# An attention and channel-mixing kernel on Trainium2: every weight chunk's first shift stays in SBUF, under a new written order

## The chip, the cores and the metric

The kernel runs on one core of a Trainium2 chip. The metric is the device time of one execution in microseconds; lower is better. The profile is one execution taken by the hardware profiler. Engines are named as it names them: PE (matrix products), PEld (its weight loads), DVE (VectorE), ACT (ScalarE), POOL (GpSimd) and SP (SyncE, which here only issues transfers).

## What is computed

The reference is windowed attention (8 batches, 8 heads, 576 positions, head size 64, each position sees itself and 63 before it), whose output feeds a mixing layer with two hidden products:

```python
scores = np.where(mask, scale * q @ k.T, -1e9)
x = softmax(scores) @ v                      # 8 x 576 x 512 after joining the heads
x_prev = x shifted by one position
xk = mu_k * x + (1 - mu_k) * x_prev
xr = mu_r * x + (1 - mu_r) * x_prev
v = np.maximum(xk @ w_k, 0) ** 2 @ w_v       # 512 -> 1024 -> 512
out = sigmoid(xr @ w_r) * v
```

The three weight matrices reach the chip as 64-bit floating-point numbers, looked at as two 32-bit words each. The kernel makes 32-bit floats of them with integer operations.

## The kernel before

Positions are cut into nine units of 512 (`u` 0 to 8, eight attention blocks of 64 positions each). A unit has four groups, one for each pair of heads (`g` is 4u plus the pair). A group runs scores on PE (`run_s`), row minima on DVE (`least`), exponentials on ACT (`exp`), reciprocals of the row sums on DVE (`shares`), the multiplication by them on DVE or POOL (`scale`), a transposition (`turn` on DVE, or a flip on PE for the first four groups), and products with the values on PE (`values`, `whole_values`). Two groups from the second unit on share one pass of `values` on PE, called a values pass below; it has 80 products. The results are copied to tile `xT`. Then `mix` blends each position with the one before (`diff`, `blend`, `seam`), and PE runs the r, k and v products of the unit.

Products with 512 columns come in two kinds. The first unit's r and k products use the decoded weight as it is (`whole`, with `xm`): one product each, which the trace shows as two MATMUL records. All others use weights and data that are each split into a rounded high part and a rest (`ws` with `xs` or `ks`): three products for each. The split is `first_part` (a cast) and `second_part` (a subtraction) for weights, `high` and `low` for data.

The weights come in 20 chunks of 128 x 512 (tile `raw`): 0 to 3 are w_r, 4 to 11 w_k, 12 to 19 w_v. `decode` handles one chunk: `sign` on ACT (absolute value of the upper words), `clamp` on DVE or POOL, then on DVE `shift` (upper word left by three bits, masked), `top` (sign and top exponent bit put back) and `low` (three bits of the lower word put in). A table `FAST` says chunk by chunk where the shift writes:

```python
def shift(e):
    words[n, 0] = words[n].bitcast(U32) if FAST[n] else bank(WC).bitcast(U32)
...
def top(e):
    shifted = words[n, 0]
    if FAST[n]:
        words[n, 0] = bank(WC).bitcast(U32)
```

With 0 the shift reads SBUF (tile `wt`) and writes a PSUM bank, and `top` works in that bank. With 1 the shift stays in `wt` in SBUF, and `top` reads `raw` and `wt`, both in SBUF, and writes the bank.

What stands where on each engine is decided while the program is built. Each step is a numbered piece; the table `ORDER` gives for each engine the numbers of the first pieces in the order in which they are to stand, for the first unit and the beginning of the second. A planner (`play`) sets the rest by keys. A piece that may run on more than one engine runs on the one in whose list it stands. So `ORDER` also moves work between engines, and it orders the transfers on SP. `PLACES` names five values passes (numbered by pair of groups, 2 to 17) ahead of which PE's instruction stream is aligned to 256 with an offset of 7, if at most `SKIP` (12) empty instructions do it.

Of the kernel before, what the change touches and what calls it, by code (L numbers as in the profile page):

```python
# [70 lines left out]
MIX = ((-90, -68, -101, -111), (-40, -47, -16, -60))  # L71
LOADS = ("q0", "w", "q1", "v0", "w", "q2", "v1", "w", "v3", "m", "q3", "v2", "w", "w", "w", "w", "w")

FAST = (0, 0, 0, 0, 0, 0, 1, 0, 0, 1, 0, 0, 0, 1, 0, 0, 0, 1, 0, 0)
MIX1 = ((-24, -66, -65, -47), (16, 60, 62, 49))

SELF = {"DVE": 125, "ACT": 140, "POOL": 100, "PE": 0, "SP": 0}
LINK = {"DVE": 125, "ACT": 135, "POOL": 90, "PE": 205, "SP": 80}
FAR_LINK = 45

PLACES, SKIP = {3: 7, 4: 7, 8: 7, 12: 7, 16: 7}, 12

RING = 8
FIRST = 730
# [4 lines left out]

ORDER = {  # L90
# [9 lines left out]
    ),  # L100
    "DVE": (
# [11 lines left out]
    ),  # L113
    "ACT": (
# [10 lines left out]
    ),  # L125
    "POOL": (
# [4 lines left out]
    ),  # L131
# [7 lines left out]
    ),  # L139
}  # L140

# [6 lines left out]
def attn_rwkv_kernel(ctx, tc, qT, kT, v2, mu_k, mu_r, w_k, w_v, w_r, out):  # L148
# [189 lines left out]
    def bank(*shape):  # L338
        return psum.tile([P, *shape], F32, name="bank")
# [81 lines left out]
    def decode(n, loaded):  # L421
# [11 lines left out]
        def shift(e):  # L433
            words[n, 0] = words[n].bitcast(U32) if FAST[n] else bank(WC).bitcast(U32)
            dve.tensor_scalar(words[n, 0], words[n].bitcast(U32), 3, 0x3FFFFFF8,
                              op0=ALU.logical_shift_left, op1=ALU.bitwise_and)
# [27 lines left out]
        p = Piece({"DVE": 335, "POOL": 605}, key, 0, clamp, [p], port=True)  # L464
        if FAST[n]:
            p = Piece("DVE", key, 335, shift, [p], port=True)
# [743 lines left out]
```

## Time and profile before

| What | us |
|---|---|
| median of three runs | 607.07 |
| lowest and highest run | 606.57, 607.09 |
| the profiled execution, its own time | 607.59 |
| its span, first to last instruction | 605.8 |
| PE busy in the span | 593.6 |
| DVE busy | 391.1 |
| ACT busy | 371.3 |
| POOL busy | 133.9 |

The span is 1.27 us less than the median of the runs and 1.8 us less than the profiled execution's own time; what lies around it is start and end of the execution. PE's records overlap their neighbours, so its busy time contains short waits within a run of products; where a products run matters, it is read from the start of one record group to the start of the next.

### The profile page before, as it was taken

The numbers are of one execution on the slowest core, as the hardware profiler recorded it, in microseconds if no ns is written. First come the engines' busy times: TensorE is split into PE (matmuls) and PEld (weight loads), VectorE is DVE, ScalarE is ACT, GpSimd is POOL, SyncE is SP. The second block draws the span as 40 slices with busy tenths as digits, with TensorE's granted clock in tenths as the row PEclk, the third lists the DMA queues.
The fourth block names the chain that finished last, engine by engine and source line by source line (L and its number), as shares of the span: only waits on it lengthen the run. The fifth ranks groups of instructions, "written<-read, shape, count | busy, mean of one in ns | idle before, by whom it ended". The sixth has DMA issues, their size and how long they took to land.

```text
span 605.8 us, 17561 instructions
## 1 busy us (share of the span) xinstructions
PE 593.6 (98%) x7008; PEld 464.7 (77%) x7008; DVE 391.1 (65%) x1210; ACT 371.3 (61%) x1057; POOL 133.9 (22%) x205
## 2 busy tenths in 40 slices
PE   5999999999999999999999999999999999999997
PEld 4644577888888888888888888887888888888885
DVE  5999999737782768366754677277828683665211
ACT  6898967475576646673577358645865476743620
POOL 6665546202300330022101130023002300201000
PEclk9999999999999999999999999999999999999999
DMA  8988133213221323122312222132212220010001
GB/s 276 320 287 282 47 88 105 80 45 107 83 77 46 93 75 97 40 82 63 110 40 57 88 83 66 41 110 81 75 46 93 92 81 24 3 53 18 0 18 52
DMA packets 56913, 53.32 MB, mean 88 GB/s; under 512 B 10496, under 2 KB 50432, under 8 KB 56832
## 3 DMA queue, kind: packets, MB, share of 16 engines
q1 hardware_dynamic: 56832, 52.20, 28.2%
q8 instruction: 56, 0.92, 0.6%
q14 instruction: 25, 0.20, 0.1%
HBM read 42.73 MB, written 9.44 MB: 86 GB/s over the span
## 4 chain that ended last, share of the span: by engine, by line
PE 84%; DVE 6%; ACT 4%; DMA 3%; SPq 1%; issue 1%; POOL 1%; ACTq 0%
PE bank L168 84%; DVE bank L168 1%; DMA raw<-w_k 1%; ACT pr L168 1%; SPq L168 1%; DMA v<-v 1%; DMA raw<-w_r 1%; DVE xm L168 1%; ACT ws L168 1%; DVE wt L168 1%; ACT kf L168 1%; DVE d L168 1%; DVE r L168 0%; DVE whole L168 0%; DVE pt L168 0%
## 5 line engine op out<-in xcount | busy, mean ns | idle before, releaser
L168 PE MATMUL bank<-xs,ws 128*128 128x512 f32 x1152 | 272.7, 396 | 0.0
L168 PEld LDWEIGHTS bank<-xs,ws 128*128 128x128 f32 x1152 | 215.8, 188 | 51.0
L168 PE MATMUL bank<-ks,ws 128*128 128x512 f32 x864 | 206.8, 398 | 0.1
L168 PEld LDWEIGHTS bank<-ks,ws 128*128 128x128 f32 x864 | 161.3, 188 | 39.5 <-issue 1.0
L168 DVE TENSOR_TENSOR ks<-kf,ks 128x512 fp32r<-128x512 f32 x70 | 51.3, 734 | 93.7 <-ACT ks L168 93.5
L168 ACT ACTIVATE pr<-pr,nmax 128x96 f32<-128x96 f32 (+1 forms) x288 | 105.2, 368 | 8.8 <-DVE nmax L168 8.3
L168 ACT ACTIVATE kf<-bank 128x512 f32<-128x512 f32 x72 | 43.0, 598 | 61.1 <-PE bank L168 60.7
L168 DVE CUSTOM_DVE_ANT_0 pr<-bank,bands 128x96 f32<-128x96 f32 x256 | 49.5, 250 | 14.3 <-PE bank L168 14.3
L168 POOL CAST ks<-kf 128x512 fp32r<-128x512 f32 x7 | 4.3, 612 | 244.9 <-ACT kf L168 206.0
L168 ACT COPY xT<-bank 128x256 f32<-128x256 f32 (+1 forms) x43 | 14.5, 392 | 67.0 <-PE bank L168 67.0
L168 ACT ACTIVATION_READ_ACCUMULATOR pr<-pr,nmax 128x1 f32 x288 | 54.5, 189 | 0.0
L168 ACT ACTIVATE kf<-kf 128x512 f32<-128x512 f32 x71 | 44.8, 633 | 2.0
L168 ACT ACTIVATE th<-bank 128x512 f32<-128x512 f32 x36 | 21.3, 591 | 38.5 <-PE bank L168 27.2
L168 DVE SCALAR_TENSOR_TENSOR r<-bank,r 128x512 f32<-128x512 f32 x36 | 24.4, 680 | 31.4 <-PE bank L168 31.3
L168 PE MATMUL bank<-xm,whole 128*128 128x512 f32 x96 | 43.1, 599 | 0.0
L168 ACT CAST ks<-kf 128x512 fp32r<-128x512 f32 x65 | 40.3, 620 | 2.1 <-POOL kf L168 0.3
L168 PE MATMUL bank<-qk 64*32 64x96 f32 (+1 forms) x2112 | 33.4, 254 | 7.8 <-DMA qk<-kT 5.2
L168 PEld LDWEIGHTS bank<-qk 64*32 64x32 f32 (+1 forms) x2112 | 28.2, 108 | 15.9 <-DMA qk<-qT 5.2
L168 PEld LDWEIGHTS bank<-pt,v 32*64 32x64 f32 (+1 forms) x2656 | 34.3, 130 | 7.0 <-issue 5.0
L168 ACT CAST xs<-d 128x512 fp32r<-128x512 f32 x49 | 28.8, 618 | 15.3 <-POOL d L168 13.7
L168 DVE TENSOR_TENSOR xs<-d,xs 128x512 fp32r<-128x512 f32 x57 | 37.3, 698 | 0.4 <-ACT xs L168 0.4
L168 DVE COPY xT<-bank 128x256 f32<-128x256 f32 x26 | 10.3, 421 | 42.2 <-PE bank L168 42.2
(79 smaller groups left out, 562.0 us busy)
## 6 DMA issues: line engine op xcount, KB each, us to landing
v<-v SPq DMA_DIRECT2D x68, 64.0 KB, 2.0
raw<-w_k SPq DMA_DIRECT2D x8, 512.0 KB, 8.4
raw<-w_v SPq DMA_DIRECT2D x8, 512.0 KB, 6.0
v<-v SPq DMA_DIRECT2D x60, 48.0 KB, 2.0
raw<-w_r SPq DMA_DIRECT2D x4, 512.0 KB, 4.8
outT<-r SPq DMA_DIRECT2D x8, 256.0 KB, 2.0
v<-v SPq DMA_DIRECT2D x60, 32.0 KB, 1.9
qk<-kT SPq DMA_DIRECT2D x8, 224.0 KB, 3.7
```

Of the source, the lines that this page charges most:

```text
L168: self.last = tc.keep_in_program_order(op(*args, **kw))
```

## The change

`FAST` is 1 for all 20 chunks instead of four of them (6, 9, 13 and 17). `ORDER` is another table for all five engines; its written part is a little longer on PE. `PLACES` names passes 3, 4, 7, 11 and 15 instead of 3, 4, 8, 12 and 16. The r and k products of the first unit keep their undivided weights (`DIRECT = "rk"` stands in both). No operation is added or taken away.

```diff
-FAST = (0, 0, 0, 0, 0, 0, 1, 0, 0, 1, 0, 0, 0, 1, 0, 0, 0, 1, 0, 0)
+FAST = (1, 1, 1, 1, 1, 1, 1, 1, 1, 1, 1, 1, 1, 1, 1, 1, 1, 1, 1, 1)
...
-PLACES, SKIP = {3: 7, 4: 7, 8: 7, 12: 7, 16: 7}, 12
+PLACES, SKIP = {3: 7, 4: 7, 7: 7, 11: 7, 15: 7}, 12
...
 ORDER = {
     "PE": (
-        509, 510, 535, 531, 566, 533, 559, 561, 557, 555, 590, 563, 1502, 1509, 1516, 1523, 588, 586, 645, 614,
+        509, 510, 535, 531, 566, 533, 559, 561, 557, 555, 590, 563, 1502, 1509, 1516, 588, 1523, 586, 645, 614,
```

Three places of the order follow. A row is one or more equal instructions of an engine, with output and inputs.

On PE, around the first values pass that two groups share (`pt,v` rows). Before:

```order
L168 MATMUL bank<-xm,whole 128x512 x9
L168 MATMUL bank<-qk 32x96 x32
L168 MATMUL bank<-xm,whole 128x512 x7
L168 MATMUL bank<-ks,ws_940 128x512 x3
L168 MATMUL bank<-xm,whole 128x512 x2
L168 MATMUL bank<-pt,v 64x96 x16
```

With the change:

```order
L169 MATMUL bank<-xm,whole 128x512 x22
L169 MATMUL bank<-qk 32x96 x32
L169 MATMUL bank<-xm,whole 128x512 x17
L169 MATMUL bank<-qk 32x96 x32
L169 MATMUL bank<-pt,v 64x96 x16
```

The scores of group 7 (the second `qk` row) now stand right ahead of that pass, and the first split product (`ks,ws`) behind it. The next values pass (groups 6 and 7) has 36 split products ahead of it before and 51 now, by a count of the rows up to it; all 48 undivided products are ahead of it in both.

On POOL, from the clamp of chunk 11 on, before (`pr` rows are `scale`, `ws` TENSOR_TENSOR rows are `second_part`, `wt` rows are `clamp`, the `ks` row is a `low` of a unit's data):

```order
L168 TENSOR_SCALAR wt<-wt 128x512
L168 TENSOR_TENSOR ws_940<-wt,ws_940 128x512
L168 TENSOR_TENSOR ks<-kf,ks 128x512
L168 TENSOR_SCALAR wt<-wt 128x512
L168 TENSOR_TENSOR pr<-pr,rs 128x384
L168 TENSOR_SCALAR wt<-wt 128x512
L168 TENSOR_TENSOR pr<-pr,rs 128x384
L168 TENSOR_SCALAR wt<-wt 128x512
L168 TENSOR_TENSOR ws_1048<-wt,ws_1048 128x512
L168 TENSOR_TENSOR ws_1052<-wt,ws_1052 128x512
L168 TENSOR_TENSOR ws_984<-whole,ws_984 128x512
L168 TENSOR_TENSOR pr<-pr,rs 128x384
```

With the change, in the same part of the program:

```order
L169 TENSOR_SCALAR wt<-wt 128x512
L169 CAST ws_950<-whole 128x512
L169 TENSOR_TENSOR pr<-pr,rs 128x384
L169 TENSOR_SCALAR wt<-wt 128x512
L169 CAST ks<-kf 128x512
L169 TENSOR_TENSOR pr<-pr,rs 128x384
L169 COPY xT<-xT 128x2
L169 TENSOR_SCALAR wt<-wt 128x512 x2
```

POOL keeps the clamps; the subtractions of this stretch are gone from it.

On DVE, in the part of the program that decodes the first w_v chunks, before:

```order
L168 SCALAR_TENSOR_TENSOR wt<-raw_715,bank 128x512
L168 TENSOR_SCALAR bank<-wt 128x512
L168 SCALAR_TENSOR_TENSOR bank<-raw_839,bank 128x512
L168 SCALAR_TENSOR_TENSOR wt<-raw_839,bank 128x512
L168 STREAM_TRANSPOSE pt<-pr 128x384
L168 TENSOR_SCALAR bank<-wt 128x512
```

With the change:

```order
L169 TENSOR_SCALAR wt<-wt 128x512
L169 TENSOR_TENSOR ks<-kf,ks 128x512
L169 SCALAR_TENSOR_TENSOR bank<-raw_789,wt 128x512
L169 TENSOR_SCALAR wt<-wt 128x512
L169 SCALAR_TENSOR_TENSOR wt<-raw_789,bank 128x512
L169 TENSOR_SCALAR wt<-wt 128x512
L169 TENSOR_TENSOR ws_1005<-wt,ws_1005 128x512
L169 TENSOR_TENSOR ks<-kf,ks 128x512
L169 STREAM_TRANSPOSE pt<-pr 128x384
L169 TENSOR_TENSOR ws_1028<-wt,ws_1028 128x512
```

The shifts now write `wt` (a clamp on DVE has the same row), `top` reads `raw` and `wt`, and the subtractions `ws` that POOL did stand among them.

## Rows read from the trace of the kernel before

**Rows 1.** The page's first part: busy us, share of the span, instructions.
```profile
PE 593.6 (98%) x7008; PEld 464.7 (77%) x7008; DVE 391.1 (65%) x1210; ACT 371.3 (61%) x1057; POOL 133.9 (22%) x205
```

**Rows 2.** The chain that ended last: start us, length us, what.
```profile
92.80 509.43 PE bank L168 x4956
```

**Rows 3.** Busy us by stretch: PE, PEld, DVE, ACT, POOL, clock, DMA share, GB/s.
```profile
11.16:81.42 70.26, 68.81 (x780) 40.00 (x788) 67.50 (x219) 65.19 (x197) 39.41 (x55) 1.00 0.72 229
...
50.00:60.00 10.00, 9.73 (x85) 4.17 (x83) 10.00 (x32) 8.39 (x22) 5.55 (x7) 1.00 0.90 294
...
300.00:350.00 50.00, 50.00 (x637) 40.69 (x636) 29.46 (x98) 31.81 (x95) 5.81 (x9) 1.00 0.24 70
```

**Rows 4.** PE in order of time: start us, length us, what, count, idle ahead.
```profile
19.84 3.70 PE L168 MATMUL bank<-xm,whole 128*128 128x512 f32 x8
...
31.17 1.00 PE L168 MATMUL bank<-qk 64*32 64x96 f32 x64 [0.23 <-ACT pt L168]
32.36 1.15 PE L168 MATMUL bank<-pt,vs 128*64 128x64 f32 x32 [0.20 <-ACT pt L168]
...
60.21 0.99 PE L168 MATMUL bank<-qk 64*32 64x96 f32 x64 [0.48 <-ACT kf L168]
...
81.31 2.06 PE L168 MATMUL bank<-pt,v 32*64 32x96 f32 x160
83.30 8.27 PE L168 MATMUL bank<-ks,ws 128*128 128x512 f32 x33
91.51 1.01 PE L168 MATMUL bank<-qk 64*32 64x96 f32 x66
...
93.70 6.53 PE L168 MATMUL bank<-ks,ws 128*128 128x512 f32 x27
100.07 22.48 PE L168 MATMUL bank<-xs,ws 128*128 128x512 f32 x96
...
135.82 1.73 PE L168 MATMUL bank<-qk 64*32 64x96 f32 x128
137.47 14.22 PE L168 MATMUL bank<-ks,ws 128*128 128x512 f32 x60
151.62 2.06 PE L168 MATMUL bank<-pt,v 32*64 32x96 f32 x160
...
423.84 1.88 PE L168 MATMUL bank<-qk 64*32 64x96 f32 x128
```

**Rows 5.** DVE by form, 11.16 to 81.42: busy us, mean ns, idle ahead, what ended it.
```profile
L168 DVE SCALAR_TENSOR_TENSOR bank<-raw,bank 128x512 uint32<-128x512 uint32 x13 | 8.9, 687 | 0.1
L168 DVE TENSOR_SCALAR bank<-wt 128x512 uint32<-128x512 uint32 x13 | 8.9, 686 | 0.8 <-POOL wt L168 0.8
...
L168 DVE SCALAR_TENSOR_TENSOR bank<-raw,wt 128x512 uint32<-128x512 uint32 x4 | 3.3, 815 | 0.0
...
L168 DVE TENSOR_TENSOR ws<-whole,ws 128x512 fp32r<-128x512 f32 x4 | 2.9, 733 | 0.0
L168 DVE TENSOR_TENSOR ks<-kf,ks 128x512 fp32r<-128x512 f32 x4 | 2.9, 720 | 0.6 <-ACT ks L168 0.5
...
L168 DVE TENSOR_SCALAR wt<-wt 128x512 uint32<-128x512 uint32 x4 | 1.7, 432 | 0.0
...
L168 DVE TENSOR_TENSOR pr<-pr,rs 128x512 f32<-128x512 f32 x2 | 1.5, 768 | 0.0
...
L168 DVE TENSOR_TENSOR pr<-pr,rs 128x384 f32<-128x384 f32 x1 | 0.6, 550 | 0.0
```

**Rows 6.** DVE in order of time, ahead of the values pass at 81.31.
```profile
77.47 1.05 DVE L168 SCALAR_TENSOR_TENSOR bank<-raw,wt 128x512 uint32<-128x512 uint32 x1
...
80.39 1.03 DVE L168 STREAM_TRANSPOSE pt<-pr 128x384 f32<-128x384 f32 x2
```

**Rows 7.** POOL in the same stretch.
```profile
77.15 0.83 POOL L168 TENSOR_TENSOR pr<-pr,rs 128x384 f32<-128x384 f32 x1 [2.74 <-DVE pt L168]
```

**Rows 8.** ACT in the same stretch.
```profile
78.36 0.62 ACT L168 CAST ws<-wt 128x512 fp32r<-128x512 f32 x1
```

77 rows, old and new, of the table ORDER are left out of this document.

## The prediction

> **What bounds the kernel now.** I read the page's first part: PE is busy for 98% of the span, no other engine for more than 65% [rows 1]. The chain that ended last shows one run of PE from 92.80 to the end of the products [rows 2]. The table of stretches shows why this is two programs: from 300 to 350 PE is busy for all of 50.00 us and DVE and ACT for 29 and 32, but from 11.16 to 81.42, where the weights are decoded, DVE is busy for 67.50 of 70.26 and ACT for 65.19, with POOL at 39.41 [rows 3]. The granted clock is 1.00 in all of them, the 2.4 GHz level. So an edit to the decoding is worth only what PE idles in the first 94 us. PE in order of time shows that idling [rows 4]. From 19.84 on it waits 0.23 and 0.20 around 31, 0.48 at 60.21 (for ACT's `kf`); 33 products from 83.30 take 8.21 to the next start, against 33 x 0.234 + 0.1 = 7.8, so 0.4; the scores from 91.51 take 2.19 to the next start, where later ones take 1.65 (135.82 to 137.47), so 0.54. Together 1.85 us. The 0.234 is 22.48 us for 96 split products. What lies ahead of 19.84 (first loads, the first softmax) has the same first rows in both orders and stays.
>
> **The point where DVE and PE meet.** I take the values pass of groups 6 and 7. PE starts it at 81.31 [rows 4]; the transpositions that make its input end at 80.39 + 1.03 = 81.42, so the second of them is just in time for the second half of the pass [rows 6]. DVE has nothing in hand there. ACT's cast ahead of it ends at 78.36 + 0.62 = 78.98 [rows 8].
>
> *PE.* By the order, 51 split products are ahead of this pass instead of 36, and all else is equal. 15 x 0.234 = 3.51. Two short passes now stand side by side, which saves one change between full products and small ones: 60 products from 137.47 to 151.62 take 14.15, and 60 x 0.234 = 14.04, so about 0.1, taken 0.15 with the other side. PE gets there at 81.31 + 3.36 = 84.67, if nothing makes it wait.
>
> *DVE.* I counted the instructions ahead of the pass in both orders and priced them by the rows by form [rows 5]; records overlap by some 0.08, which I take off each mean. Added: 3 `scale` of 512 (0.69 each) 2.07, 4 of 384 (0.47) 1.88, 3 `second_part` (0.65) 1.95, 3 `low` of data (0.64) 1.92, 2 clamps (the trace has no quiet clamp of their form; the nearest row is the shift in `wt`, 0.35) 0.70; one `blend` more and two copies of `xT` less cancel about. Gained: 4 shifts in `wt` and 13 into a bank become 18 in `wt`: 18 x 0.35 - 4 x 0.35 - 13 x 0.61 = -3.03. So the shifts do get 0.25 us shorter each. The 13 `top`s that change form: the row mean is 0.815 for `raw,wt` and 0.687 for `raw,bank`, a bound of 13 x 0.13 = 1.7; one of the four took 1.05 beside POOL [rows 6], the other three have a mean of (3.26 - 1.05)/3 = 0.737, which gives 0.65; the lower bound is nothing. I take 0.3, since POOL has less work. Sum: 8.52 - 3.03 + 0.3 = +5.8, between 5.5 and 7.2.
>
> *What DVE gets back.* POOL has 18 instructions fewer ahead of the pass (6 `second_part`, 7 `scale`, 2 casts, the rest single ones). At 39.41/55 = 0.72 [rows 3] that is 13 us, a third. DVE's idle time is 70.26 - 67.50 = 2.76, of which 0.8 is for POOL's `wt` [rows 5]; a third of it is 0.9. A `top` was stretched from 0.74 to 1.05; 0.3 in 3.3 us of the four is 9%. Some 25 us of DVE's busy time are forms with two inputs from SBUF; a third of 9% of that is 0.7. Taken 1.6, between 0 and 2.8.
>
> DVE is ready at 81.42 + 5.8 - 1.6 = 85.6, PE at 84.67: PE waits 0.95 there. With the ends of the bounds it is between 0 and 4.0 (7.2 and nothing back: 88.6).
>
> *ACT.* 4 casts, 2 `xm` multiplications, one `sign` and 2 copies more, some 0.5 each: +4.4, which makes 78.98 + 4.4 = 83.4, 1.3 ahead of PE: hidden. If DVE's work were not late there, ACT would be next, with that 1.3 in hand.
>
> *The other idle times of PE.* The 0.43 at the flips stays. The 0.48 for `kf`: the first split product now stands behind a values pass of 1.99, not ahead of it, so ACT has more time; taken 0.2, bounds 0 and 0.5. The 0.4 from 83.30 on lies where POOL made a `ks`; it is now DVE's: taken 0, bounds 0 and 0.4. The 0.54 at 91.51: half, 0.3. Sum 0.43 + 0.2 + 0.95 + 0 + 0.3 = 1.88, against 1.85.
>
> *Loads.* On SP, the load of chunk 9 is moved behind those of chunks 13, 10, 11 and 17. By sizes 13.1 MB instead of 10.1 are ahead of it, at 294 GB/s in the busiest stretch [rows 3] 10 us later. Its `sign` on ACT also stands 13 steps later, about 10 us, so I cost the move at nothing; that cover is worth 2 to 3 us if it is thinner than that. The other loads move by a place or two.
>
> *`PLACES`.* The trace shows score passes of two lengths: 1.73 and, in six passes, 1.88 (423.84) [rows 4]. Which one a pass gets may hang on where the instructions lie. 6 x 0.15 = 0.9 either way is the bound; no row says which passes will be long, so I take 0.
>
> **Sum.** +0.03 of waits, -0.15 for the change between kinds: -0.1. Span 605.8 - 0.1 = 605.7. The median of the runs is 1.27 above that span (the profiled execution itself 1.8), so 605.7 + 1.27 = 606.9 us. I call "no change" what is within 0.2%, 1.2 us, about what a measurement of this kernel can tell.
>
> **A rule against the change.** What the row shows: POOL's multiplication ran from 77.15 to 77.98 [rows 7], the `top` that began in it at 77.47 ended at 78.52 instead of about 78.2 [rows 6]; three others without such a neighbour took 0.74. The Trainium skill, page "SBUF — State Buffer", section "Who interferes with whom", says that DVE and GpSimd share one pair of SBUF ports as an exclusive lock, and that the later of two operations which want it blocks until the first is done. By that rule the `top` would have started anew at 77.98 and ended at 78.67; the trace has 78.52, which agrees within 0.15. It speaks against putting both inputs of `top` in SBUF: that is rival C.
>
> **Rivals.**
> - A, the forecast: waits are moved, not removed. 606.9; its own range 605.9 to 608.1. For it: DVE's added work (5.8) and PE's added work ahead of the pass (3.4) are of like size. Chance 0.48.
> - B, faster: DVE gets back 2.6 or more and PE never waits at that pass, and the 0.48, 0.4 and 0.54 go to 0.1 in all. Then 0.53 of waits are left of 1.85, and with -0.15 it is -1.5, up to -2.0 if the flips' waits shrink too: 605.1 to 605.6. For it: DVE sheds 0.25 us on each of 13 shifts and POOL a third of its work. Against it: the trace shows no DVE slack at 81.4. Chance 0.30.
> - C, slower: DVE and POOL collide. 14 shifts and 13 `top`s come to have all of their operands in SBUF. POOL keeps 26 of 72 us, and half an instruction of it is 0.36 us: 27 x 0.36 x (26/72) = 3.5 us in place of 0.3, so that PE waits 0.95 + 3.2 = 4.1, or 2.5 if half of the relief still comes: 1.5 to 3.2 above A, 608.4 to 610.1. It decides from a wait of 2.3 us at the pass. Against it: the four shifts that already stay in `wt` have a mean of 0.43 [rows 5], so they were hardly stopped. Chance 0.15.
> - D, slower: chunk 9's load lands late. ACT's `sign` waits 2 to 3 us, DVE behind it idles, and PE with it: some 1 to 1.5 over A after the slack of 1.3: about 608.3. Chance 0.07.
>
> The range 605.0 to 608.8 leaves out the end of C and the rest of B with a long gain of `PLACES`, less than 2 in 10. Faster 0.30, same 0.48, slower 0.22 come from B, from A, and from C and D.
>
> **What would show it.** Right: DVE's shifts near 0.43 and none above 0.6, PE's start of the pass of groups 6 and 7 near 85.6 with a wait of about 1 us for DVE; 1.5 to 2.3 us of PE idle in all from 19.84 on; the unbroken run from there to the end as long as the products make it. Wrong: a pass at 84.7 or earlier without a wait (B), `top`s with a mean over 0.9 that begin inside POOL instructions (C), an idle ACT ahead of a `sign` that a transfer ends (D), or score passes of another length from 130 us on (`PLACES`).

## The result and the profile after

The changed kernel takes 610.85 us (median of five runs, 610.16 to 613.91), against 607.07 before: the ratio is 1.0073, 95% interval 1.0053 to 1.0093. It is slower by 3.8 us by the medians (4.4 by the ratio; the five runs spread over 3.8); the forecast was 606.9 and a range up to 608.8. The profiled execution has a span of 609.0 us, 3.2 more than before. The page's first part:

```profile
PE 594.1 (98%) x7008; PEld 465.9 (76%) x7008; DVE 392.6 (64%) x1225; ACT 373.0 (61%) x1062; POOL 111.4 (18%) x185
```

Beside [rows 1], POOL lost 22 us of work and no engine gained much. The loss must be in places. I read the chain that ended last first; its columns are start, length and what:

```profile
33.32 52.74 PE bank L169 x434
86.06 0.21 issue
86.27 1.82 PE bank L169 x85
88.09 1.41 issue
89.50 82.44 PE bank L169 x866
171.95 0.48 issue
172.43 433.03 PE bank L169 x4185
```

Before, the last unbroken run of PE began at 92.80 [rows 2]. Now PE is on the path from 33.32 on. DVE, ACT and POOL hold it up nowhere behind that; what interrupts it is "issue", which is time in which the engine waited for nothing that the profile shows. PE in order of time:

```profile
21.77 2.84 PE L169 MATMUL bank<-xm,whole 128*128 128x512 f32 x6
...
74.34 11.71 PE L169 MATMUL bank<-ks,ws 128*128 128x512 f32 x48
86.27 1.82 PE L169 MATMUL bank<-pt,v 32*64 32x96 f32 x123 [0.21 <-issue]
89.50 0.71 PE L169 MATMUL bank<-pt,v 32*64 32x96 f32 x37 [1.41 <-issue]
90.14 3.76 PE L169 MATMUL bank<-ks,ws 128*128 128x512 f32 x15
...
170.23 1.72 PE L169 MATMUL bank<-qk 64*32 64x96 f32 x126
172.43 0.32 PE L169 MATMUL bank<-qk 64*32 64x96 f32 x2 [0.48 <-issue]
172.68 3.52 PE L169 MATMUL bank<-xs,ws 128*128 128x512 f32 x14
```

Two things differ from [rows 4]. The first whole product starts at 21.77 instead of 19.84: 1.93 us are lost before any of the places that the prediction looked at. And PE stops inside two passes of small products. The values pass of groups 6 and 7 takes 3.87 from 86.27 to 90.14 instead of 1.99, and the score pass at 170.23 takes 2.44 to the next start instead of 1.66: 1.88 + 0.78 = 2.66 us. Together 4.6 against 3.2 of the spans; the other 1.4 come back, as PE's waits for other engines behind 20 us are gone.

The start. DVE of the kernel before, in order of time:

```profile
5.13 0.55 DVE L168 TENSOR_SCALAR wt<-wt 128x512 f32<-128x512 f32 x1 [5.13 <-ACT wt L168]
5.72 0.70 DVE L168 TENSOR_SCALAR bank<-wt 128x512 uint32<-128x512 uint32 x1
6.54 0.29 DVE L168 CUSTOM_DVE_ANT_0 pr<-bank,mask 128x128 f32<-128x128 f32 x1
```

DVE of the kernel after, whose first instruction this is:

```profile
8.58 0.43 DVE L169 TENSOR_SCALAR wt<-wt 128x512 uint32<-128x512 uint32 x1 [8.58 <-POOL wt L169]
8.93 0.28 DVE L169 CUSTOM_DVE_ANT_0 pr<-bank,mask 128x128 f32<-128x128 f32 x1
```

POOL of the kernel after, ahead of it:

```profile
5.32 2.52 POOL L169 TENSOR_SCALAR_AFFINE_SELECT bands<-bands 32x96 f32<-32x96 f32 x8
7.94 0.61 POOL L169 TENSOR_SCALAR wt<-wt 128x512 f32<-128x512 f32 x1
```

Before, DVE clamps chunk 0 itself at 5.13 and starts the first row minima (`CUSTOM_DVE_ANT_0`) at 6.54. In the new order that clamp stands on POOL, behind the eight mask instructions. DVE's first instruction is the shift of chunk 0, which needs the clamp; the minima stand behind the shift in DVE's queue and start at 8.93, 2.4 us later. The scores that they need were there in time.

The decoding itself, DVE by form from 11 to 90 us:

```profile
L169 DVE SCALAR_TENSOR_TENSOR bank<-raw,wt 128x512 uint32<-128x512 uint32 x17 | 11.8, 694 | 0.0
...
L169 DVE TENSOR_SCALAR wt<-wt 128x512 uint32<-128x512 uint32 x19 | 8.0, 424 | 0.9 <-POOL wt L169 0.7
```

A shift takes 0.424 and a `top` 0.694, against 0.815 for that form in [rows 5]: no collisions to speak of. ACT's waits from 11 to 100 us name no transfer, where the kernel before waited 1.6 and 0.9 us for `raw`: rival D did not happen.

### The profile page after: what moved, and what is told of

Read it like the earlier page. It is cut to its first block, busy times and chain, and to the rows that moved or that the text cites. A ratio compares the mean times of both kernels' runs of the same rounds, so it can differ in the third digit from the quotient of the medians.

```text
span 609.0 us, 17563 instructions
## 1 busy us (share of the span) xinstructions
PE 594.1 (98%) x7008; PEld 465.9 (76%) x7008; DVE 392.6 (64%) x1225; ACT 373.0 (61%) x1062; POOL 111.4 (18%) x185
## 4 chain that ended last, share of the span: by engine, by line
PE 96%; DMA 2%; DVE 1%; issue 1%; POOL 0%; SPq 0%; POOLq 0%
PE bank L169 96%; DMA raw<-w_r 2%; DMA qks<-qT 1%; DVE pr L169 0%; DVE mu L169 0%; DVE r L169 0%; DVE bank L169 0%; DVE pt L169 0%; POOL pr L169 0%; SPq L169 0%; DVE wt L169 0%; DVE rs L169 0%; DVE nmax L169 0%; POOL xT L169 0%; POOLq L169 0%
## 5 line engine op out<-in xcount | busy, mean ns | idle before, releaser
L169 ACT CAST ks<-kf 128x512 fp32r<-128x512 f32 x63 | 38.9, 619 | 1.8
L169 PE MATMUL bank<-pt,v 32*64 32x96 f32 (+3 forms) x2656 | 37.3, 244 | 1.6 <-issue 1.6
L169 DVE COPY xT<-bank 128x256 f32<-128x256 f32 x23 | 9.0, 422 | 44.1 <-PE bank L169 44.1
```

Source lines behind the costliest of these rows:

```text
L169: self.last = tc.keep_in_program_order(op(*args, **kw))
```

## The experiments

All times are medians on the chip, each beside runs of the kernel before on the same chip (607.16, 607.17 and 607.45 in the three sets).

### First set: the clamp, the alignment, and FAST by itself

The first clamp (piece 6) back at the head of DVE's list:

```diff
     "DVE": (
-        7, 511, 513,
+        6, 7, 511, 513,
...
     "POOL": (
-        643, 6, 520, 10,
+        643, 520, 10,
```

> The kernel after, with the first clamp (chunk 0) at the head of DVE's list, as before the change, in place of POOL's behind the band masks. Theory 1 (that clamp delays DVE's first minima by 2.4 us and PE by 1.9): first whole product near 19.9 instead of 21.77, time 1.9 below the kernel after, about 608.9. Rival (the new order of the first loads on SP is what is late): no more than 0.5 below it, about 610.4.

Measured: 608.56, ratio to before 1.0028 (1.0015 to 1.0041), 2.3 below the kernel after. Its DVE in order of time:

```profile
5.09 0.89 DVE L169 TENSOR_SCALAR wt<-wt 128x512 f32<-128x512 f32 x2 [5.09 <-ACT wt L169]
6.71 0.29 DVE L169 CUSTOM_DVE_ANT_0 pr<-bank,mask 128x128 f32<-128x128 f32 x1 [0.73 <-PE bank L169]
```

The minima now wait for PE's scores, not for POOL, and the first whole product starts at 19.76. The rival (the loads) falls: the loads stand as in the kernel after. PE's stops are still there, with 1.01 and 0.20 us somewhat shorter.

No alignment of PE's instructions at all:

```diff
-PLACES, SKIP = {3: 7, 4: 7, 7: 7, 11: 7, 15: 7}, 12
+PLACES, SKIP = {}, 12
```

> The kernel after without any alignment of PE's instruction stream (PLACES empty). Theory 2 (in the values pass at 86.27 and the score pass at 170.23 PE stands still for the next 16 KB of its own instructions, because both begin just behind the start of such a piece): the instruction stream lies elsewhere, the two stops of 1.41 and 0.48 us go or move, time 1.5 to 2.7 below the kernel after, 608.2 to 609.4. Rival (the stop in the values pass is work of DVE or ACT that the profile doesn't name): stops as in the kernel after, same time, 610.9.

Measured: 615.17, 1.0130 (1.0111 to 1.0149): a miss in the size and the sign, 4.3 above the kernel after, and the most useful run of all. The two stops are gone, and there are three others. PE in order of time:

```profile
183.88 2.05 PE L169 MATMUL bank<-pt,v 32*64 32x96 f32 x159
187.34 0.18 PE L169 MATMUL bank<-pt,v 32*64 32x32 f32 x1 [1.42 <-issue]
...
345.36 1.98 PE L169 MATMUL bank<-pt,v 32*64 32x96 f32 x151
349.19 0.32 PE L169 MATMUL bank<-pt,v 32*64 32x32 f32 x9 [1.85 <-issue]
...
509.19 1.94 PE L169 MATMUL bank<-pt,v 32*64 32x96 f32 x143
512.74 0.38 PE L169 MATMUL bank<-pt,v 32*64 32x96 f32 x17 [1.61 <-issue]
```

They are in values passes 6, 11 and 16, each 8 records sooner in its pass than the last one (159, 151, 143), and each 4096 instructions behind the last one, counted in all records of PE and PEld, waits with them, that had begun when PE stopped. So the places are set by where an instruction lies. The page's part on queues has 55 packets of instructions with 0.90 MB in queue 8 of this run, some 16 KB each, and PE has 14149 records (7008 MATMULs, 7008 weight loads, 133 waits and the like): 257 to a packet, close to the 256 that the alignment names. I call 256 instructions a piece.

From the order I counted the place of each pass in PE's instructions: two for a split product or a transposition, four for the others (two MATMUL and two weight loads), and one for each wait that stands as an instruction. One constant is free, where the program begins in a piece; the stop in pass 6 sets it (63). Then the same count gives the other places, with no further choice:

| kernel, pass | start in its piece | a piece ends after (instructions of the pass) | PE stopped after |
|---|---|---|---|
| no alignment, pass 6 | 193 | 63 and 319 | 318 (sets the constant) |
| no alignment, pass 11 | 209 | 47 and 303 | 302 |
| no alignment, pass 16 | 224 | 32 and 288 | 286 |
| after, pass 3 | 7, behind 252 empty | 249 | 246 |
| after, score pass at 170.23 | 255 | 1 and 257 | 252 |

(A row's MATMUL count times two is the last column.) The rule that I read from it: PE stops where a second piece ends inside a pass of small products, because the piece behind it was asked for too late. A values pass has 320 instructions in 2.0 us, so it can use up a piece in 1.6 us.

That PE waits there for its instructions is also in the traces' records of transfers. In all twelve stops inside passes, in six kernels, a packet of queue 8 lands 1.2 to 1.5 us before PE goes on: at 185.89 for the start at 187.34, at 347.75 for 349.19, at 88.13 for 89.50 in the kernel after. That one in the queue's row from 86.9 to 88.2 us (packets, MB, share):

```profile
q8 instruction: 1, 0.02, 5.7%
```

The rule is not complete. By the same count pass 7 of the run without alignment starts at 247, and a second piece ends after 265 of its instructions, yet PE goes through it without a stop, in both kernels without alignment:

```profile
217.40 2.07 PE L169 MATMUL bank<-pt,v 32*64 32x96 f32 x160
```

There the last packet ahead of that place had landed at 215.36, 2.0 us before the pass began. What counts is when the packet lands, and the count by itself doesn't give that.

The stop in pass 3 of the kernel after needs more than the count. The pass would stand at 11 in its piece, where only one end (245) lies in it; the alignment to 7 moves it on by 252 instructions, nearly a piece, and at 7 there is also one end. What the alignment puts there is in the trace: for each pass named in `PLACES` PE's sequencer, which issues its instructions (PEldq in the rows), has one COMPARE_BRANCH at the line of `addr_align`, and none in the run without alignment. Before, after, and a run of the second set in which pass 3 is aligned by 252 again (shortest, median and longest in ns):

```profile
L666 PEldq COMPARE_BRANCH  x5: 275/280/309, 77.1 to 499.6; - x5
...
L667 PEldq COMPARE_BRANCH  x5: 275/289/4278, 81.9 to 470.9; - x5
...
L667 PEldq COMPARE_BRANCH  x4: 275/288/3811, 80.4 to 435.8; - x4
```

So a place is aligned also where more than `SKIP` empty instructions are needed, and what I wrote of `SKIP` ahead of the prediction (no alignment then) does not hold. The empty instructions have no records; their numbers stay a count, and the count needs the 252, and 191 ahead of pass 4, for the score pass to come out. They don't seem to be worked off one by one: the branches with 129 (before) and 191 (after) of them took 0.28 and 0.29 us. The long branch is the one with 252, ahead of pass 3, from 81.93 to 86.21: a packet lands in it at 84.75, PE works off what it has and starts the pass at 86.27, and the next packet, at 88.13, is late as well. Whether the length of that step or its place right behind the start of a piece makes the branch long, these runs don't tell apart.

A stop has a second price. Busy us by stretch of the run without alignment (the columns of [rows 3]):

```profile
348.00:351.00 3.00, 1.81 (x15) 1.50 (x15) 1.56 (x4) 1.09 (x3) 0.00 (x0) 0.92 0.31 85
351.00:354.00 3.00, 3.00 (x9) 2.33 (x8) 1.21 (x2) 2.62 (x5) 1.48 (x3) 0.51 0.21 56
354.00:357.00 3.00, 3.00 (x15) 2.43 (x14) 2.96 (x5) 0.96 (x3) 1.47 (x2) 1.00 0.29 97
```

Behind the stop the granted clock is 0.51, the 1.2 GHz level, for some 3 us: 9 products where the next stretch has 15. So I estimate one stop at some 1.6 us, or 3 with the six products lost behind it; without alignment the kernel takes 6.8 us more than with the places of the second set (615.17 and 608.35), for three stops.

Both edits together (the two diffs above):

> Both edits on the kernel after: first clamp on DVE, PLACES empty. If theories 1 and 2 hold and add up: 610.9 - 1.9 - 2.2 = 606.8, between 606.0 and 607.5. If a wait for DVE takes the place of the stops (rival C of the prediction, collisions of DVE and POOL): 608.0 or more, with idle time of PE ended by DVE between 60 and 95 us.

Measured: 613.48, 1.0109 (1.0077 to 1.0140). The sum fails with its second part: the three stops of the run above are there too, at the same instructions.

`FAST` by itself, in the old order:

```diff
-FAST = (0, 0, 0, 0, 0, 0, 1, 0, 0, 1, 0, 0, 0, 1, 0, 0, 0, 1, 0, 0)
+FAST = (1, 1, 1, 1, 1, 1, 1, 1, 1, 1, 1, 1, 1, 1, 1, 1, 1, 1, 1, 1)
```

> The kernel before with FAST 1 for all chunks and nothing else (its own ORDER and PLACES). If the shifts in SBUF are a gain by themselves, DVE is 2 to 3 us earlier at the values pass of groups 6 and 7 and PE loses less of the 1.85 us: 0.5 to 1.2 below before, 605.9 to 606.6. Rival C (shift and top collide with POOL's work, which is not smaller here): 1 to 3 us above before, with tops of a mean over 0.9 us.

Measured: 622.88, 1.0259 (1.0240 to 1.0277): 15.7 us slower, five times what I gave rival C at most. DVE by form, 11 to 90 us:

```profile
L168 DVE SCALAR_TENSOR_TENSOR bank<-raw,wt 128x512 uint32<-128x512 uint32 x17 | 16.3, 956 | 0.1
L168 DVE TENSOR_SCALAR wt<-wt 128x512 uint32<-128x512 uint32 x17 | 12.9, 757 | 2.4 <-POOL wt L168 2.4
```

The shift in SBUF is slower here (0.757) than the one into a bank was (0.686, [rows 5]), and `top` takes 0.956. Taken one by one in this trace, the 13 shifts that overlap a POOL instruction have a mean of 0.862, the other four 0.416; of the `top`s ten have 1.147 and the other seven 0.683. Before, the shifts into a bank took 0.687, all of them beside POOL. So POOL's neighbourhood is the cause of the slow ones. `FAST` does a second thing: the planner makes POOL wait for a shift and a `top` with all operands in SBUF, so this edit also brings 32 such pieces into an order made without them.

### Second set: places chosen by the count

`PLACES` such that no second piece ends in any pass and no more than 70 empty instructions stand ahead of one, with the clamp on DVE:

```diff
-PLACES, SKIP = {3: 7, 4: 7, 7: 7, 11: 7, 15: 7}, 12
+PLACES, SKIP = {6: 7, 10: 7, 14: 7}, 12
```

> The kernel after with the first clamp on DVE and PLACES naming passes 6, 10 and 14 alone. Counted from the order, no pass of scores or values then starts so that a second piece of 256 instructions begins inside it, and none has more than 70 empty instructions ahead of it. Theory 2, as the last runs leave it (PE stands still where two pieces begin in one pass, or where a piece of nearly only empty instructions stands ahead of one): no stop of PE over 0.3 us from 35 us on, time 608.6 - 1.3 - 0.5 - 0.5 = 606.3, below before by 0.8. Rival (a wait for DVE takes the stop's place at the values pass of groups 6 and 7, as the prediction had it): 607.2 or more, with PE idle there for DVE.

Measured: 607.16, 0.9997 (0.9988 to 1.0006). No stop is left and none for DVE takes its place; the chain ends with two runs of PE:

```profile
16.96 73.40 PE bank L169 x813
90.36 510.67 PE bank L169 x4984
```

But the time equals that of before, 0.9 above what I expected. The profiled executions would give more: from the first whole product to the last product 581.4 us here and 582.4 before. The medians don't have that 1.0, and the interval leaves at most 0.7: the two profiled executions lie on either side of what is usual, before at 607.59 and here at 606.49, for medians of 607.17 and 607.16. So the kernels are equal although PE's waits for other engines (1.85 by the prediction's reading) are gone; what takes these back is open.

The same `PLACES` on the kernel after, its clamp left on POOL (the diff above, and no other):

> The same PLACES on the kernel after, with the first clamp left on POOL behind the masks. Theory 1: the first whole product at 21.8 and 1.9 us more than the run with the clamp on DVE, 608.2. Rival (DVE's late start is caught up, since DVE and not PE's start sets the values passes): less than 1 us more.

Measured: 608.35, 1.0019 (1.0010 to 1.0028): 1.2 more, between theory and rival. In the profiles the first whole product is 2.1 later (21.78 and 19.66), as is the span nearly (606.4 and 604.6).

Pass 3 in `PLACES` again, which brings back the branch over 252 instructions (and makes the one ahead of pass 6 step over 74 for 70):

```diff
-PLACES, SKIP = {6: 7, 10: 7, 14: 7}, 12
+PLACES, SKIP = {3: 7, 6: 7, 10: 7, 14: 7}, 12
```

> As the first kernel of this set, with pass 3 named in PLACES again, which is one more piece nearly full of empty instructions (252) ahead of that pass and nothing else that matters (pass 6 then needs 74 for 70). Theory 2: a stop of 1 to 1.5 us in the values pass of groups 6 and 7, and 1.3 to 2.4 us more than the first kernel, about 608.0. Rival (the stop in the kernel after came from another place): no stop, same time as the first kernel.

Measured: 608.35, 1.0022 (1.0012 to 1.0032), 1.2 more. The branch ahead of pass 3 takes 3.81 us (its row stands in the first set), and there is one stop, at the same instruction as in the kernel after:

```profile
84.42 1.81 PE L169 MATMUL bank<-pt,v 32*64 32x96 f32 x123
87.20 0.71 PE L169 MATMUL bank<-pt,v 32*64 32x96 f32 x37 [0.98 <-issue]
```

The clamp's move alone, on the kernel before:

```diff
     "DVE": (
-        6, 7, 511, 513,
+        7, 511, 513,
...
     "POOL": (
-        643, 520, 10,
+        643, 6, 520, 10,
```

> The kernel before with its first clamp on POOL behind the masks, where the change puts it, and nothing else. Theory 1: DVE's first minima at 8.9 instead of 6.5, the first whole product about 1.9 later than 19.84, time 1.5 to 2.4 above before, about 609.0. Rival (the kernel before has its own slack there): within 0.5 of before.

Measured: 608.89, 1.0030 (1.0019 to 1.0042), 1.7 above before. DVE's first instruction is again the shift, at 8.58, and the first whole product starts at 22.08.

### Third set: what keeps the shifts short

The shifts of ten chunks back in banks, on the kernel with the clamp on DVE and the new places (607.16):

```diff
-FAST = (1, 1, 1, 1, 1, 1, 1, 1, 1, 1, 1, 1, 1, 1, 1, 1, 1, 1, 1, 1)
+FAST = (0, 0, 0, 0, 0, 0, 1, 1, 1, 1, 0, 1, 1, 1, 0, 0, 0, 1, 1, 1)
```

> The new order with the first clamp on DVE and PLACES 6, 10, 14 (607.2 in the last runs), with the shifts of chunks 0 to 5, 10, 14, 15 and 16 back in PSUM banks (as many of the 16 as the order can hold). Theory 3 (what the change gained in the decoding is the shift, 0.25 us each): DVE needs 10 x 0.25 = 2.5 us more ahead of the values pass of groups 6 and 7, PE waits for DVE there and before, time 1.0 to 2.5 above, 608.2 to 609.7. Rival (the new order leaves DVE that much in hand, the shift's place is worth nothing by itself): 607.2, within 0.6.

Measured: 609.32, 1.0029 (1.0019 to 1.0038), 1.9 more by the ratios. PE's waits from 20 us on name ACT's `kf`:

```profile
PE bank L169 <- ACT kf L169: 0.7, 2, 0.5
```

I had expected waits for DVE; these are for ACT. The ten shifts' place is worth about 2 us in this order, together with the waits of POOL for these shifts and their `top`s, which the edit takes away too; where the 2 us are lost, these waits (0.7) don't show in full.

POOL no longer held behind the DVE instructions that want SBUF alone; the order of all engines stays:

```diff
-BOUND = 125000
+BOUND = 0
```

> The same kernel without the ordering that makes POOL's instructions wait for the last DVE instruction which uses SBUF alone (BOUND 0; the order on every engine is the same). Theory 4 (DVE's shifts and tops stay short in the new order since POOL is held behind them): shifts with a mean of 0.55 and tops of 0.8 or more, and 2 to 8 us more, 609 to 615. Rival (they are short since POOL has little work): shifts under 0.46, tops under 0.74, time within 0.6 of 607.2.

Measured: 611.71, 1.0068 (1.0055 to 1.0081), 4.3 more by the ratios (1.0068 and 0.9997). `top` and shift, 11 to 90 us:

```profile
L169 DVE SCALAR_TENSOR_TENSOR bank<-raw,wt 128x512 uint32<-128x512 uint32 x17 | 13.4, 786 | 0.0
L169 DVE TENSOR_SCALAR wt<-wt 128x512 uint32<-128x512 uint32 x18 | 9.3, 524 | 0.0
```

0.524 for 0.423, and 0.786 for 0.708: a little under what I had named, the time inside the range. Beside a POOL instruction ran 8 of the 18 shifts (0.666, the others 0.410) and 10 of the 17 `top`s (0.857, the others 0.684); with the waits it was 4 of 19 of either. It is the waiting of POOL that keeps them short.

The same edit (`BOUND` 0) on `FAST` by itself in the old order:

> The kernel before with FAST 1 for all (622.9 in the first set), without the ordering that makes POOL wait. Theory 4a (the 15.7 us are collisions of DVE and POOL in SBUF): still 616 or more, shifts over 0.6 and tops over 0.85 in the mean. Rival 4b (they are waits of POOL for DVE that the 16 more held instructions bring into an order made without them): 607 to 612, and shifts near 0.43.

Measured: 614.91, 1.0122 (1.0109 to 1.0135), which is neither: about half of the 15.7 us goes with the waits, and with a shift of 0.682 and a `top` of 0.976 the collisions stay. Both theories hold for a part.

And the new places on the kernel before, whose pass 3 then starts at 233 in its piece:

```diff
-PLACES, SKIP = {3: 7, 4: 7, 8: 7, 12: 7, 16: 7}, 12
+PLACES, SKIP = {6: 7, 10: 7, 14: 7}, 12
```

> The kernel before with PLACES naming passes 6, 10 and 14 alone. By the count of theory 2, pass 3 then starts 23 instructions ahead of the end of a piece and meets a second end 279 in; no other pass does. Theory 2: one stop of PE of 1 to 2 us near the end of the values pass of groups 6 and 7 (81 to 85 us), time 1.2 to 2.4 above before, 608.4 to 609.6. Rival (these stops belong to the new order): no stop, within 0.5 of before.

Measured: 608.78, 1.0037 (1.0018 to 1.0057). One stop, after 278 instructions of the pass where the count says 279:

```profile
80.82 2.03 PE L168 MATMUL bank<-pt,v 32*64 32x96 f32 x139
84.37 0.47 PE L168 MATMUL bank<-pt,v 32*64 32x96 f32 x21 [1.52 <-issue]
```

So these stops belong to no order; they come from where a pass lies, and the places that the kernel before names keep it free of this one (1.3 us by this pair).

## Why the prediction was wrong

The 3.8 us are accounted for: the clamp's move back takes 2.3 off, the new places take 2.5 off (610.85 to 608.35), both together 3.7 (607.16), so the two overlap by some 1.1. What is left of the change, `FAST` and the new order, is what the prediction argued about, and there it said 606.9 where 607.2 was measured. That this part comes so near is luck in good part: the forecast moved PE's waits to the pass of groups 6 and 7, and there is no wait there, and no gain either. Two steps failed.

- "What lies ahead of 19.84 ... has the same first rows in both orders and stays." True of PE, false of DVE and POOL: the clamp of chunk 0 changed its engine, and DVE waits for it with all of the first group's minima behind. Price 1.2 to 2.3 us, by the pair of runs taken. I had compared PE's rows alone there, and begun DVE's count at 11.16.
- The term for `PLACES`, "so I take 0", with a bound of 0.9 from two lengths of score passes. The bound was from the wrong effect: those two lengths stand in every run, whatever `PLACES` says. What it governs is stops of 0.2 to 1.9 us with a low clock behind some of them: 1.4 us by one pair of runs, 2.5 by the other. Range and rivals had no such case.

Point by point, the rest:

- **PE at the values pass.** Forecast 84.67 without waits. With the clamp on DVE and no stops it starts at 83.61; the 3.36 us more of work are right, and 0.9 of earlier waits, which I had left in, are gone.
- **DVE there.** Forecast 85.6; the last transposition ends at 82.75 + 1.03 = 83.78 in that kernel, again just in time for the pass. So the wait of 0.95 isn't there. The instructions got the lengths that I took (shift 0.423, `top` 0.708 for 0.71). Up to that point DVE's busy time rose by 4.5 us (72.49 to 76.95) for the forecast 5.8 less 0.7, and its idle time fell by 2.1 (8.93 to 6.83) for the forecast 0.9: together 2.4 later, not 4.2.
- **Rival B** was right on the waits (none of PE's from 34 us on is for DVE, ACT or POOL) and wrong on the time.
- **Rival C** was right on the mechanism and wrong for this order. The Trainium skill, page "SBUF — State Buffer", section "Who interferes with whom", says that of two operations of DVE and GpSimd that want the shared port pair, the later one blocks; a shift of 0.757 in place of 0.424, in the same stretch and with 42 us of POOL's work for 24, agrees. Here the planner makes POOL wait, and the new order gives it less to do: without the first, 4.3 us are lost.
- **Rival D** fell: ACT waits for no transfer. (The 294 GB/s taken for it are not the busiest stretch: from 10 to 20 us the kernel before moved 338.)

## What to carry to other kernels

Read a reordering from the first instruction on, on every engine: what moved to another engine, and what stands ahead of it there and behind its reader. A faster form of an operation and the order around it are one change; alone, this one cost 15.7 us. Where runs of very short instructions stand on an engine, ask where its instruction stream is cut, and read a stop that no semaphore explains ("issue") by its place in that stream and by the packet of instructions that lands ahead of its end. "Issue" by itself doesn't name this cause: PE's 0.46 at 74.83 in the run of `FAST` without POOL's waits has the same mark, and the last packet had landed 8 us before.

## What the runs showed of the hardware

- PE stopped for 0.2 to 1.9 us inside passes of small products, at instructions that a count by 256 names to within 1 to 5, in six kernels, and went on 1.2 to 1.5 us after a packet of instructions had landed. The Trainium skill, page "Runtime: NRT & Kernel Launch", section "Instruction fetch mechanics", describes a refill in blocks of 16 KiB or 256 instructions, which agrees with the packets and the 4096 instructions between the stops; it also says that this is hidden since instructions are issued more slowly than they are fetched, and that the cost of crossing a block is mostly hidden. Here it was not, where a second block ended inside a pass at 320 instructions in 2.0 us, with one exception (pass 7 without alignment).
- An alignment of PE's instructions is one COMPARE_BRANCH in the trace. It took 0.28 to 0.31 us where the count gives 30 to 191 empty instructions, and 3.8 to 4.5 in the three kernels where it gives 252; with the stop behind it that cost 1.2 us (607.16 to 608.35).
- A shift of 128x512 with input and output in SBUF took 0.416 us by itself and 0.862 where it overlapped a POOL instruction; one into a PSUM bank took 0.687 beside POOL.
- After some of these stops the granted clock was 0.5 for about 3 us (0.51 from 351 to 354), after others it stayed at 1.00 (the stop at 88.09 of the kernel after). One kernel's runs then spread: 609.8 to 617.9 in the one with both edits of the first set.
